# Batch 1's values loaded, copied and mixed earlier, and the third attention product ahead of the transposes

## The chip, the core and the metric

The kernel runs on one core of one Trainium2 chip. A core has a matrix engine (TensorE, PE in the profile; its weight loads are shown as PEld), a vector engine (VectorE, DVE), an activation engine (ScalarE, ACT), a general engine (GpSimd, POOL) and a queue engine (SyncE, SP). Each has its own instruction queue, and they wait for each other by semaphores. Transfers between device memory and on-chip memory are issued from SP's and POOL's queues and run on 16 DMA engines. The metric is the device time of one execution in microseconds, as the median over several runs. The time before is 253.93 us, the median of 9 runs (253.62 to 256.23).

## The reference: what is computed

Inputs are `q`, `k`, `v` of shape (4 batches, 8 heads, 768 positions, 64), a sorting matrix of 8x8 per batch and head, and three weights of an FFN (512 to 1536, gate and value, and 1536 to 512).

1. The 8x8 matrices are made nearly doubly stochastic by five rounds of: exponential, division by row sums, division by column sums. Call the result P.
2. The 768 positions are 8 blocks of 96. Keys and values are mixed over blocks: block i of the sorted keys is the sum over j of P[i,j] times block j, likewise for the values.
3. Each block of queries attends to the sorted keys and values of its own block: softmax(scale * q k^T) v, 96x96 scores per block and head.
4. The heads are laid side by side to x, 3072 tokens by 512, and the result is `(silu(x w_gate) * (x w_val)) w_out`, in float32.

## The kernel before, in words

Matrices are held in bfloat16; weights, keys, values and most queries are loaded and cast in one go by DMAs that POOL issues (`load_k`, `load_q`, `load_v`, `load_gv`, the latter two slices of 256 columns of gate and value weights). The order of those DMA issues is POOL's program order. POOL also does copies: `copy_v` rearranges a quarter of a batch's values in `v_tiles` to `vch`, with the head dimension outermost. Batches 0 and 1 share one such tile: batch 0 in the lower 64 partitions (`lowr`), batch 1 in the upper (`highr`). Batches 2 and 3 load into the same memory later, so their loads wait until batch 0's and batch 1's copies are done.

The mixing by P is done on PE: `kq_chunk` (matmuls at L235, tile `tkq`) multiplies 8 or 16 position columns of keys and queries at once by `rmix`, which also transposes them, and `v_chunk` (L247, tile `tv`) does the same for the values out of `vch`, by `vmix`. A value chunk covers a range of the head dimension and all 96 positions, so it needs all four quarters of the copy. Each chunk lands in a PSUM bank and is drained to on-chip memory by DVE ("v") or ACT ("s"), as its call names. PSUM tags are "a" and "b" (pairs of banks), "x" (one bank) and "gen" (a ring of three).

A unit of attention is two heads and four blocks: `qk` (scores L278, exponentials on ACT L291 or L289), `av` (L305, then a reciprocal and a product on DVE, L309 and L311, into `st`), and `x_to` (transposes, L322), drained into `xt`. A batch has 8 units; four units make one half batch of 384 tokens.

The FFN runs in 8 passes, one per half batch (`ffn(n)`). A pass has 12 chunks m of 128 hidden columns: `gate(n, m)` (L356, four matmuls of 384 columns), a tanh on ACT (L364) and a product on DVE (L366); `value(n, m)` (L374) and a product on DVE (L379); and, for the pass before it, three output projections `outp(n-1, t3, part)` (L391) of 128 tokens in three parts of four matmuls.

The order of PE and POOL is written out by hand. Until the first pass a straight list of calls is used: fillers on a zero tile (`fill`, L417), batch 0's value chunks, its key and query chunks, the four units of its first half with fillers between, and the first FFN matmuls taken apart by `early(n, kcs)` (L507: n = 0 and 1 are gate 0 and value 0, n = 2 is gate 1). From then on `merge(main, side)` walks through a pass's calls, adds up their costs (0.65 per gate or value, 0.87 per output part), and inserts a side call as soon as the sum reaches the number written beside it. `kqs`, `vs` and `units` make these side lists for a later half batch. DVE and ACT are also in written order until the first pass; after that a scheduler places them.

In the second pass (`ffn(1)`) the side work is batch 1's: three pairs of key and query chunks, four value chunks, then its first four units.

The rows behind `copy_v` for batch 1 on POOL are, before the change: `load_k_pair()` (keys of batches 2 and 3, into the buffer of batch 0's keys), the four copies, `load_v(2)`, `load_v(3)`, and two query casts into device memory (`q_cast`).

Of the kernel before, what the change touches and what calls it, by code (L numbers as in the profile page):

```python
# [17 lines left out]
def kernel(  # L18
# [15 lines left out]
    C = S // NB  # L34
# [5 lines left out]
    DF = moe_w_gate.shape[1]  # L40
    NKC = DM // 128
# [47 lines left out]
    def load_k(b, lo, hi):  # L89
        nc.gpsimd.dma_start(out=kq_tile(b)[0:R, lo:hi, :], in_=k_nat[b, :, lo:hi, :])  # L90

    def load_k_pair():
        kq_tiles["p"] = natp.tile([128, C, D], BF16, name="kp", tag="nat")
        for u in range(2):
            nc.gpsimd.dma_start(out=kq_tiles["p"][u * R:(u + 1) * R], in_=k_nat[2 + u])
# [4 lines left out]
    def load_v(b, lo, hi):  # L100
        if b // 2 not in v_tiles:
            v_tiles[b // 2] = vnp.tile([128, C, D], BF16, name=f"v{b // 2}", tag="vn")
        u = b % 2
        nc.gpsimd.dma_start(out=v_tiles[b // 2][u * R:(u + 1) * R, lo:hi], in_=v_nat[b, :, lo:hi, :])

    def load_w(sb, dram, lo, hi):
        nc.gpsimd.dma_start(out=sb[:, :, lo:hi], in_=dram[:, :, lo:hi])  # L107

    def load_gv(lo, hi):
        load_w(wg_sb, wg_dram, lo, hi)  # L110
        load_w(wv_sb, wv_dram, lo, hi)

    def copy_v(eng, pair, rows, s, n=4):
        cs = slice(s * (C // n), (s + 1) * (C // n))
        dst = vch3[rows, :, cs]
        src = v_tiles[pair][rows, cs, :]
        if eng is nc.scalar:
            eng.copy(dst, src.transpose([0, 2, 1]))
        else:
            eng.tensor_copy(dst, src.transpose([0, 2, 1]))  # L120
# [16 lines left out]
    copy_v(nc.gpsimd, 0, lowr, 3)  # L137
    landed = const.tile([R, 1], BF16)
    nc.gpsimd.tensor_copy(landed, kq_tiles[0][0:R, C - 1, D - 1:D])
    for m in range(0, DF, 256):  # L140
        load_gv(m, m + 256)
    load_k(1, 0, C)
    load_v(1, 0, C)
    load_q(1, 0, C)
    nc.gpsimd.dma_start(out=wo_sb, in_=wo_dram)

# [30 lines left out]
    def pair_tile(name, tag):  # L177
        return psum.tile([128, 1024], FP32, name=name, tag=tag)
# [24 lines left out]
    for lo in (0, NB // 2):  # L203
        part = slice(lo, lo + NB // 2)
# [89 lines left out]
    def qk(b, u, tag="b"):  # L294
        exps(b, u, *scores(b, u, tag))

    def av(b, u, tag="a"):
        half, g = divmod(u, H2)
        vt = vts[b // 2][:, b % 2].rearrange("p (h i) e -> p h i e", h=H)
        av_ps = pair_tile("av_ps", tag).rearrange("p (two n) -> p two n", two=2)  # L300
        o = av_ps[:, :, 0:4 * (D + 1)].rearrange("p two (i e) -> p two i e", e=D + 1)
        for two in range(2):
            e = es[(b, u)][two]
            for i4 in range(4):
                nc.tensor.matmul(o[:, two, i4, :], lhsT=e[:, i4 * C:i4 * C + 128],  # L305
                                 rhs=vt[:, 2 * g + two, half * 4 + i4, :],
                                 start=True, stop=True)
        r_sb = ssp.tile([C, 2, 4, 1], FP32, name="r_sb", tag="r")
        nc.vector.reciprocal(r_sb, o[0:C, :, :, D:D + 1])  # L309
        st = ssp.tile([C, 4, 2, D], BF16, name="st", tag="st")  # L310
        nc.vector.tensor_tensor(st.rearrange("p i two d -> p two i d"), o[0:C, :, :, 0:D],  # L311
                                r_sb.to_broadcast([C, 2, 4, D]), op=ALU.mult)
        sts[(b, u)] = st

    def xt_tile(tag, n):
        bank = psum.tile([128, 1024], BF16, name="x_ps", tag=tag, bufs=3 if tag == "gen" else 1)
        return bank[:, 0:n * 4 * C].rearrange("p (g a b) -> p g a b", g=n, b=C)
# [66 lines left out]
    def outp(n, t3, part):  # L384
        b, half = divmod(n, 2)
        h_w = h_tiles[n]
        if part == 0:
            o_tiles[n] = bank_tile("o_ps", "x" if 2 <= n < 2 * B - 1 or n == 2 * B - 1 and t3 == 1 else "gen")
        o_ps = o_tiles[n]
        for m in range(part * 4, part * 4 + 4):  # L390
            nc.tensor.matmul(o_ps, lhsT=h_w[:, m, ts(t3, 128)], rhs=wo_sb[:, m, :],  # L391
                             start=(m == 0), stop=(m == NFC - 1))
        if part < 2:
            return
        o_sb = opool.tile([128, DM], FP32, name="o_sb", tag="o_sb")
        nc.scalar.copy(o_sb, o_ps)  # L396
        base = b * S + half * TW + t3 * 128
        nc.sync.dma_start(out=out[ds(base, 128), :], in_=o_sb)
# [14 lines left out]
    idle_ps = bank_tile("idle_ps", "x")  # L413

    def fill(tile, n):
        for _ in range(n):
            nc.tensor.matmul(tile, lhsT=warm_sb[:, 0:128], rhs=warm_sb, start=True, stop=True)  # L417
# [37 lines left out]
    fill(idle_ps, 2)  # L455
    v_chunk(0, 0, 8, "v", "gen")
    v_chunk(0, 8, 16, "s", "a")
    fill(idle_ps, 2)
    v_chunk(0, 24, 16, "v", "b")
    fill(idle_ps, 2)  # L460
    v_chunk(0, 40, 8, "s", "gen")
    v_chunk(0, 48, 8, "v", "gen")
    v_chunk(0, 56, 8, "s", "gen")
# [17 lines left out]
    idle_ps = bank_tile("idle_ps")  # L481
# [3 lines left out]
    av(0, 1, "b")  # L485
    fill(idle_ps, 1)
    xts[(0, 0)] = xtp.tile([128, H2, TW], BF16, name="xt0_0", tag="xt")
    x01 = xt_tile("x", 2)
    x_to(x01[:, 0], 0, 0)
    fill(idle_ps, 1)  # L490
    qk(0, 3, "gen")
    av(0, 2, "a")
    x_to(x01[:, 1], 0, 1)
    drain("s", xts[(0, 0)][:, 0:2, :], x01.rearrange("p g a b -> p g (a b)"))
    fill(idle_ps, 2)
    av(0, 3, "b")
    x2 = xt_tile("gen", 1)
    x_to(x2[:, 0], 0, 2)
# [3 lines left out]
    def early(n, kcs):  # L502
        sb, m, name = ((wg_sb, 0, "g_ps"), (wv_sb, 0, "v_ps"), (wg_sb, 1, "g_ps"))[n]
        if n not in first:
            first[n] = psum.tile([128, TW], FP32, name=name, tag="gen", bufs=3)
        for kc in kcs:
            nc.tensor.matmul(first[n], lhsT=sb[:, kc, ts(m, 128)], rhs=xts[(0, 0)][:, kc, :],  # L507
                             start=(kc == 0), stop=(kc == NKC - 1))

    early(0, (0,))  # L510
    early(1, (0,))
    x3 = xt_tile("x", 1)
    x_to(x3[:, 0], 0, 3)
    drain("v", xts[(0, 0)][:, 3:4, :], x3.rearrange("p g a b -> p g (a b)"))
    early(0, (1, 2))
    early(1, (1, 2))
    early(0, (3,))
    early(1, (3,))
    early(2, range(NKC))
    gate_out(0, 0, first[0])  # L520
    value_out(0, 0, first[1])
    gate_out(0, 1, first[2])
# [5 lines left out]
    def units(b, us, ats):  # L528
        us = list(us)
        todo = []  # L530
        for n, at in enumerate(ats):
            u, u2 = us[2 * n:2 * n + 2]
            held = []
            todo.append((at, lambda u=u, u2=u2, held=held: (qk(b, u, "b"), held.append(scores(b, u2, "a")))))
            todo.append((at + 1.3, lambda u2=u2, held=held: exps(b, u2, *held[0])))
            for w, tag, t in ((u, "b", 1.9), (u2, "a", 3.6)):
                if b < 2:
                    todo.append((at + t, lambda w=w, tag=tag: av(b, w, tag)))
                    todo.append((at + t + 3.1, lambda w=w: drain("v", *xtr(b, w))))
                else:  # L540
                    todo.append((at + t, lambda w=w, tag=tag: (av(b, w, tag), x_dma(b, w))))
        return todo

    def kqs(b, ats):
        return [(at, lambda n=n: (kq_chunk(b, n * 32, 16, "v", "b"), kq_chunk(b, n * 32 + 16, 16, "s", "a")))
                for n, at in enumerate(ats)]

    def vs(f, size, ats):
        return [(at, lambda m=m: f(1, m * size, size, "sv"[m % 2], "ba"[m % 2])) for m, at in enumerate(ats)]

    def merge(main, side):
        done, k = 0.0, 0
        side = sorted(side, key=lambda t: t[0])
        for c, f in main:
            f()
            done += c
            while k < len(side) and side[k][0] <= done:
                side[k][1]()
                k += 1
        while k < len(side):  # L560
            side[k][1]()
            k += 1

    def ffn(n):
        todo = []
        for m in range(NFC):
            if n > 0 or m > 1:
                todo.append((0.65, lambda m=m: gate(n, m)))
            if n > 0 or m > 0:
                todo.append((0.65, lambda m=m: value(n, m)))  # L570
            if n > 0 and m % 4 == 3:
                for part in range(3):
                    todo.append((0.87, lambda m=m, part=part: outp(n - 1, m // 4, part)))
        return todo

    load_k_pair()
    for s in range(4):
        copy_v(nc.gpsimd, 0, highr, s)
    load_v(2, 0, C)
    load_v(3, 0, C)  # L580
    q_cast(2)
    q_cast(3)
    both = slice(0, 128)
    merge(ffn(0), units(0, range(4, 8), (0.0, 5.6)))
    merge(ffn(1), kqs(1, (0.3, 2.6, 4.9)) + vs(v_chunk, 16, (6.2, 7.3, 8.4, 9.5)) + units(1, range(4), (11.0, 15.6)))
    for s in range(4):
        copy_v(nc.gpsimd, 1, both, s)
    nc.vector.memset(kqt_tile("p")[:, 2 * GI * C:], 0.0)
# [42 lines left out]
```

The softmax here doesn't subtract the row's maximum and nothing guards it: scores larger than these inputs give would overflow.

## Time and profile before

The profiled execution took 254.17 us; the span from its first to its last instruction is 252.1 us, at a granted TensorE clock of 0.999 of full speed.

| engine | busy us | share of the span |
|---|---|---|
| PE | 238.3 | 95% |
| PEld | 143.2 | 57% |
| DVE | 159.4 | 63% |
| ACT | 110.6 | 44% |
| POOL | 51.9 | 21% |

The stages on PE, in us from the span's start: batch 0's value chunks 12.8 to 16.0, its key and query chunks 16.0 to 20.7, the first four units and the early FFN matmuls 21.6 to 30.3, the first pass from there to 47.5, the second pass 47.5 to 80.8, and six further passes and the last projections to 249.

Times of single instructions are "start, length"; matmuls are pipelined, so a group's length holds the latency of its last one, and the distance from one start to the next tells more (four matmuls of 384 columns go by in 0.65 us, four of 512 in 0.87, a key chunk of 64 matmuls in 1.13). An idle time in brackets is that of the engine just before the instruction, with what ended it; "issue" means that nothing shown by the profile did. For a DMA the trace gives the time of its issue and how long after that it landed. Some matmul records are missing, and a short idle time between fillers is mostly a missing filler.

### The profile page before, as it was taken

How to read it: one execution, taken by the hardware profiler on the slowest of the kernel's cores; microseconds unless marked ns; L12 is line 12 of the kernel's file. 1: busy time of each engine (PE TensorE's matmuls, PEld its weight loads, DVE VectorE, ACT ScalarE, POOL GpSimd, SP SyncE). 2: the span in 40 equal slices, each digit the busy share in tenths (PEclk: the TensorE clock that was granted, in tenths of full speed). 3: DMA queues.
4: the chain of work that ended last, by engine and by line, in shares of the span. 5: the costliest groups of instructions: out<-in, count | busy, mean ns of one | idle time of the engine just before them, and what ended most of it. 6: DMA issues, size and time to landing. Idle time of an engine off the chain costs nothing.

```text
span 252.1 us, 6035 instructions
## 1 busy us (share of the span) xinstructions
PE 238.3 (95%) x2548; PEld 143.2 (57%) x2574; DVE 159.4 (63%) x342; ACT 110.6 (44%) x187; POOL 51.9 (21%) x46
## 2 busy tenths in 40 slices
PE   5698799999999999999999999999999999999994
PEld 5275456566555565656656555555655565555543
DVE  6768588875756856758668457545854585456700
ACT  2965454346442443455543533443444343332311
POOL 7847430899069100000000000000000000000000
PEclk9999999999999999999999999999999999999999
DMA  6959999999999176110113122111211111100122
GB/s 104 210 96 159 197 219 219 189 221 218 223 158 144 42 175 123 44 42 3 42 26 80 42 51 52 46 44 33 61 56 42 34 57 57 44 11 30 44 83 85
DMA packets 37866, 23.98 MB, mean 95 GB/s; under 512 B 26064, under 2 KB 34000, under 8 KB 37328
## 3 DMA queue, kind: packets, MB, share of 16 engines
q0 software_dynamic: 21328, 14.16, 38.3%
q1 hardware_dynamic: 16512, 9.45, 13.0%
q8 instruction: 20, 0.33, 0.5%
q14 instruction: 6, 0.05, 0.1%
HBM read 28.32 MB, written 7.86 MB: 144 GB/s over the span
## 4 chain that ended last, share of the span: by engine, by line
PE 74%; DMA 15%; DVE 3%; POOL 3%; issue 2%; ACT 1%; DVEq 0%; POOLq 0%
PE o_ps L391 23%; PE v_ps L374 21%; PE g_ps L356 20%; DMA kq<-in_q_dram 7%; DMA kq<-in_k_dram 4%; DMA wg_sb<-in_moe_w_gate_dram 4%; PE tkq L235 3%; PE av_ps L305 2%; PE qk L278 2%; PE tv L257 1%; DVE gs_sb L366 1%; PE o_ps L407 1%; DVE vt L213 1%; POOL wg_sb L107 1%; POOL wv_sb L107 1%
## 5 line engine op out<-in xcount | busy, mean ns | idle before, releaser
L366 DVE SCALAR_TENSOR_TENSOR gs_sb<-th_sb,g_ps 128x384 bf16<-128x384 bf16 x96 | 52.8, 550 | 52.9 <-ACT th_sb L364 50.7
L374 PE MATMUL v_ps<-xt,wv_sb 128*128 128x384 bf16 x380 | 77.3, 326 | 0.3
L356 PE MATMUL g_ps<-xt,wg_sb 128*128 128x384 bf16 x376 | 76.5, 326 | 0.0
L364 ACT ACTIVATE th_sb<-g_ps 128x384 bf16<-128x384 f32 x96 | 47.1, 491 | 58.0 <-PE g_ps L356 54.9
L391 PE MATMUL o_ps<-wo_sb,h 128*128 128x512 bf16 x256 | 62.2, 379 | 1.1
L379 DVE SCALAR_TENSOR_TENSOR h<-v_ps,gs_sb 128x384 bf16<-128x384 f32 x96 | 53.3, 555 | 6.9 <-DVE gs_sb L366 0.5
L374 PEld LDWEIGHTS <-wv_sb 128*128 128x128 bf16 x380 | 35.4, 97 | 23.6 <-issue 1.5
L356 PEld LDWEIGHTS <-wg_sb 128*128 128x128 bf16 x376 | 34.6, 97 | 22.9 <-issue 0.2
L391 PEld LDWEIGHTS <-h 128*128 128x128 bf16 x276 | 26.0, 98 | 27.7
L396 ACT COPY o_sb<-o_ps 128x512 f32<-128x512 f32 x23 | 13.5, 585 | 51.4 <-PE o_ps L391 51.4
L120 POOL COPY vch<-v 64x1536 bf16<-64x1536 bf16 (+1 forms) x10 | 28.1, 2845 | 18.6 <-DMA v<-in_v_dram 10.4
L291 ACT ACTIVATE e_all<-qk 96x768 bf16<-96x768 f32 x30 | 22.5, 802 | 6.2 <-PE qk L278 6.2
L311 DVE TENSOR_TENSOR st<-av_ps,r_sb 96x512 bf16<-96x512 f32 x32 | 21.7, 679 | 0.2
L305 PEld LDWEIGHTS <-e_all 96*128 96x128 bf16 x256 | 12.2, 98 | 5.1 <-ACT e_all L291 0.9
L305 PE MATMUL av_ps<-vt,e_all 96*128 96x65 bf16 x256 | 13.5, 194 | 0.2 <-ACT e_all L291 0.2
L213 DVE CAST vt<-tv 96x1024 bf16<-96x1024 f32 (+1 forms) x9 | 9.8, 1101 | 4.3 <-PE tv L247 4.3
L215 ACT CAST vt<-tv 96x1024 bf16<-96x1024 f32 (+1 forms) x9 | 9.1, 1029 | 5.6 <-PE tv L247 2.9
L309 DVE RECIPROCAL r_sb<-av_ps 96x8 f32<-96x8 f32 x32 | 6.4, 199 | 7.1 <-PE av_ps L305 7.1
L235 PE MATMUL tkq<-rmix,kq 128*64 128x64 bf16 x384 | 7.6, 197 | 1.1 <-DMA kq<-in_q_dram 0.6
L215 ACT CAST kqt<-tkq 128x1024 bf16<-128x1024 f32 (+1 forms) x7 | 6.0, 894 | 5.7 <-PE tkq L235 5.7
L213 DVE CAST kqt<-tkq 128x1024 bf16<-128x1024 f32 (+1 forms) x7 | 7.5, 1070 | 1.2 <-PE tkq L235 1.1
L235 PEld LDWEIGHTS <-kq 128*64 128x64 bf16 x384 | 6.7, 113 | 2.4 <-issue 2.2
(79 smaller groups left out, 135.9 us busy)
## 6 DMA issues: line engine op xcount, KB each, us to landing
out_dram<-o_sb SPq DMA_DIRECT2D x23, 256.0 KB, 2.0
v<-in_v_dram POOLq DMA_DIRECT2D x3, 768.0 KB, 14.1
kq<-in_q_dram POOLq DMA_DIRECT2D x2, 768.0 KB, 13.4
wg_sb<-in_moe_w_gate_dram POOLq DMA_DIRECT2D x6, 256.0 KB, 9.6
wv_sb<-in_moe_w_val_dram POOLq DMA_DIRECT2D x6, 256.0 KB, 10.2
wo_sb<-in_moe_w_out_dram POOLq DMA_DIRECT2D x1, 1536.0 KB, 23.7
kp<-in_k_dram POOLq DMA_DIRECT2D x2, 768.0 KB, 27.0
q_scr<-in_q_dram POOLq DMA_DIRECT2D x2, 768.0 KB, 20.9
```

The costliest lines, as they stand in the source:

```text
L120: eng.tensor_copy(dst, src.transpose([0, 2, 1]))
L213: nc.vector.tensor_copy(dst, src)
L235: nc.tensor.matmul(tp[two * D:(two + 1) * D, lc, :], lhsT=kq_tiles[b][:, at + lc, :], rhs=rm[:, two, :], start=True, stop=True)
L291: nc.scalar.activation(e_all[:, n:n + 2, 0:4 * C], wide[0:C, :, 0:4 * C], AF.Exp, scale=scale)
L305: nc.tensor.matmul(o[:, two, i4, :], lhsT=e[:, i4 * C:i4 * C + 128], rhs=vt[:, 2 * g + two, half * 4 + i4, :], start=True, stop=True)
L311: nc.vector.tensor_tensor(st.rearrange("p i two d -> p two i d"), o[0:C, :, :, 0:D], r_sb.to_broadcast([C, 2, 4, D]), op=ALU.mult)
L356: nc.tensor.matmul(g_ps, lhsT=wg_sb[:, kc, ts(m, 128)], rhs=xt[:, kc, :], start=(kc == 0), stop=(kc == NKC - 1))
L364: nc.scalar.activation(th_sb, g_ps, AF.Tanh, scale=0.5)
L366: nc.vector.scalar_tensor_tensor(gs_sb, th_sb, 1.0, g_ps, op0=ALU.add, op1=ALU.mult)
L374: nc.tensor.matmul(v_ps, lhsT=wv_sb[:, kc, ts(m, 128)], rhs=xt[:, kc, :], start=(kc == 0), stop=(kc == NKC - 1))
L379: nc.vector.scalar_tensor_tensor(h_tiles[n][:, m, :], v_ps, 0.5, gs_tiles.pop(m), op0=ALU.mult, op1=ALU.mult)
L391: nc.tensor.matmul(o_ps, lhsT=h_w[:, m, ts(t3, 128)], rhs=wo_sb[:, m, :], start=(m == 0), stop=(m == NFC - 1))
```

## The change

On POOL, batch 1's value load moves from behind the third key load to ahead of the last two pairs of weight slices (the last four of twelve weight DMAs), and the four copies move ahead of `load_k_pair()`. On PE, six fillers go: four among batch 0's value chunks and two among the first units. The scores of unit 3 and the third `av` move ahead of the first transposes. The early FFN matmuls are taken in another order: two contraction chunks of gate 0 and value 0 ahead of the last transposes, one of gate 1 between the others. In the second pass the value chunks come first and the key and query chunks after them, the units start 0.3 and 0.2 later in the list's costs, and the output projections of the first half batch follow chunks 5, 8 and 11 instead of 3, 7 and 11.

```diff
     nc.gpsimd.tensor_copy(landed, kq_tiles[0][0:R, C - 1, D - 1:D])
-    for m in range(0, DF, 256):
+    for m in range(0, 1024, 256):
+        load_gv(m, m + 256)
+    load_v(1, 0, C)
+    for m in range(1024, DF, 256):
         load_gv(m, m + 256)
     load_k(1, 0, C)
-    load_v(1, 0, C)
     load_q(1, 0, C)
     nc.gpsimd.dma_start(out=wo_sb, in_=wo_dram)
...
     v_chunk(0, 0, 8, "v", "gen")
     v_chunk(0, 8, 16, "s", "a")
-    fill(idle_ps, 2)
     v_chunk(0, 24, 16, "v", "b")
-    fill(idle_ps, 2)
     v_chunk(0, 40, 8, "s", "gen")
...
     xts[(0, 0)] = xtp.tile([128, H2, TW], BF16, name="xt0_0", tag="xt")
+    qk(0, 3, "gen")
+    av(0, 2, "a")
     x01 = xt_tile("x", 2)
     x_to(x01[:, 0], 0, 0)
-    fill(idle_ps, 1)
-    qk(0, 3, "gen")
-    av(0, 2, "a")
     x_to(x01[:, 1], 0, 1)
     drain("s", xts[(0, 0)][:, 0:2, :], x01.rearrange("p g a b -> p g (a b)"))
-    fill(idle_ps, 2)
+    fill(idle_ps, 1)
     av(0, 3, "b")
...
-    early(0, (0,))
-    early(1, (0,))
+    early(0, (0, 1))
+    early(1, (0, 1))
     x3 = xt_tile("x", 1)
     x_to(x3[:, 0], 0, 3)
     drain("v", xts[(0, 0)][:, 3:4, :], x3.rearrange("p g a b -> p g (a b)"))
-    early(0, (1, 2))
-    early(1, (1, 2))
+    early(0, (2,))
+    early(1, (2,))
+    early(2, (0,))
     early(0, (3,))
     early(1, (3,))
-    early(2, range(NKC))
+    early(2, (1, 2, 3))
...
-            if n > 0 and m % 4 == 3:
+            ends = (5, 8, 11) if n == 1 else (3, 7, 11)
+            if n > 0 and m in ends:
                 for part in range(3):
-                    todo.append((0.87, lambda m=m, part=part: outp(n - 1, m // 4, part)))
+                    todo.append((0.87, lambda t3=ends.index(m), part=part: outp(n - 1, t3, part)))
...
-    load_k_pair()
     for s in range(4):
         copy_v(nc.gpsimd, 0, highr, s)
+    load_k_pair()
     load_v(2, 0, C)
...
-    merge(ffn(1), kqs(1, (0.3, 2.6, 4.9)) + vs(v_chunk, 16, (6.2, 7.3, 8.4, 9.5)) + units(1, range(4), (11.0, 15.6)))
+    merge(ffn(1), vs(v_chunk, 16, (2.2, 3.1, 4.0, 4.9)) + kqs(1, (5.8, 8.0, 10.2)) + units(1, range(4), (11.3, 15.8)))
```

## The prediction, made before the changed kernel was run

> **What bounds the kernel now.** I read the page's busy line first, then busy time by stage, then TensorE's (PE's) timeline where a stage holds less work than it lasts, then the waits and GpSimd's (POOL's) timeline.
>
> The page's first line, then the stages (us, busy time per engine, granted clock, DMA share, GB/s):
>
> ```profile
> PE 238.3 (95%) x2548; PEld 143.2 (57%) x2574; DVE 159.4 (63%) x342; ACT 110.6 (44%) x187; POOL 51.9 (21%) x46
> ...
> 12.60:16.00 3.40, 3.11 (x68) 2.26 (x68) 1.91 (x3) 1.77 (x4) 0.12 (x1) 1.00 0.65 123
> 16.00:21.60 5.60, 4.93 (x198) 3.94 (x199) 4.52 (x7) 3.88 (x6) 5.60 (x9) 1.00 0.81 97
> 21.60:30.30 8.70, 6.90 (x99) 4.20 (x101) 5.14 (x16) 4.90 (x9) 4.44 (x7) 1.00 1.40 189
> 30.30:47.40 17.10, 16.96 (x165) 10.57 (x164) 14.93 (x35) 8.07 (x15) 4.89 (x5) 1.00 1.17 209
> 47.40:80.80 33.40, 32.33 (x468) 20.27 (x470) 23.61 (x44) 14.78 (x24) 24.98 (x12) 1.00 1.48 200
> 80.80:252.00 171.20, 166.87 (x1416) 97.16 (x1431) 100.69 (x196) 69.15 (x121) 1.86 (x1) 1.00 0.19 53
> ```
>
> From 30.3 on PE is the bound: the end moves by as much as the first full pass starts earlier, less what is lost later. Only the stages before 80.8 are changed. In 12.6 to 30.3 much of PE's time is filler; this is where most can be won. The attention start:
>
> ```profile
> 25.07 0.43 PE L305 MATMUL av_ps<-vt,e_all 96*128 96x65 bf16 x8
> 25.34 0.24 PE L322 MATMUL x_ps<-ident,st 96*128 96x96 bf16 x2
> 26.52 0.26 PE L322 MATMUL x_ps<-ident,st 96*128 96x96 bf16 x2 [0.94 <-issue]
> 26.61 0.60 PE L417 MATMUL idle_ps<-warm_sb 128*128 128x512 bf16 x2
> 27.05 0.42 PE L305 MATMUL av_ps<-vt,e_all 96*128 96x65 bf16 x8
> ...
> q8 instruction: 1, 0.02, 5.4%
> ```
>
> PE stops in the middle of four transposes whose data is there, released by nothing (issue). The last line, the DMA view of 24.2 to 25.3 alone, shows a packet of PE's code starting then; the page has 20 such of 16 KB for PE's 5,161 instructions, so one per 256. I read the stop as PE out of code. Waits in 47 to 81, and the four second-half copies on POOL:
>
> ```profile
> PE tkq L235 <- DMA kq<-in_q_dram: 0.6, 1, 0.6
> PE qk L278 <- DVE vt L213: 0.3, 1, 0.3
> ...
> 45.11 11.24 POOL L120 COPY vch<-v 64x1536 bf16<-64x1536 bf16 x4 [9.63 <-DMA v<-in_v_dram]
> ```
>
> **Part 1, up to the first scores.** Four fillers between the value chunks go. Two such (14.68) take 0.54 to the next chunk's start at 15.22, the first pair 0.69 (an idle 0.16 in it): 1.23 together. The key chunks then wait for bank "a", whose ScalarE (ACT) drain runs 13.68 + 1.06 = 14.74; so they start at 14.8 instead of 16.02: **1.2**. All later drains follow PE at the same distance, so the 1.2 lasts to the third AV. Key loads are not in the way: the last lands at 15.83, and its chunk (19.78) comes at 18.5. Bounds: 0.7 (the first pair alone) to 1.6 (if an extra 0.25 idle at 17.2 and at 19.5 shrinks too).
>
> **Part 2, third AV ahead of x.** Before, the first matmul of plain FFN order (L374) starts at 30.30; the fourth AV starts 0.53 after the stop ends (26.52 to 27.05: half a transpose group, two fillers), and L374 3.25 after that. Counting 256 instructions on from the stop's place, the next block of code again ends inside this group, now two matmuls into the fourth AV, with transposes and third AV already behind it; so the 0.53 goes. From the fourth AV on: its last transposes start +1.44 (27.05 to 28.49), the key matmuls behind their drain +0.83 (28.49 to 29.32), then five matmuls at 0.163 = 0.82: 3.09 instead of 3.25, 0.16 won. If the code arrives 1.2 earlier too, because its request was made 1.2 earlier: 1.2 + 0.53 + 0.16 = **1.9** for parts 1 and 2. Bounds: code no earlier than now, since the queues carry the same weights then: 0.7. No stop at all: the AV waits for the exps, which start 0.37 after the scores (24.80 to 25.17) and take 0.86; scores now at 23.1 (third exps end 24.26 - 1.2), AV 24.4, L374 27.5: 2.8. I take 1.9, the value nearest the one stop the trace has.
>
> The Trainium skill ("Runtime: NRT & Kernel Launch", Instruction fetch mechanics) says code comes in 16 KiB blocks, PE's store holds 2048 instructions and a block's crossing is mostly hidden. The 0.94 row contradicts the last point; by the rule alone there would be no stop afterwards and the sum would be the 2.8 case, near 251.0.
>
> **Part 3, loads.** On POOL's queue the ninth issue (21.96) and each later one wait for the landing eight before; single issues landed at 21.7, 23.0, 24.5, 26.8, 28.0, 29.4, 30.6, 32.0 (weights), 33.3, 34.6, 36.1, 38.0, then third key 41.0, value 45.0, query 48.7, output weights 55.9. They land in issue order; so the moved value load takes its 3.0 to 4.0 at 32.0 and lands at 35 to 36; the last four weight slices land up to 4.0 later (37.3, 38.6, 40.1, 42.0), the key at 45, query and output weights unchanged. First needs before: gate 8 at 41.53, value 8 at 42.17, gate 10 at 44.56, value 10 at 45.35; less 1.9: 39.6, 40.3, 42.7, 43.4. Each covered, by 1.4 at the least; cost 0. Copies 36 to 47.3 (11.24). The pair load, two values and two query casts that queue behind the copies on POOL are issued from 47.3, while output weights are in flight to 55.9: the queue never empties, cost 0. VectorE (DVE) beside copies: L366 means 550 ns in 45.2 to 56.3, 545 in 31 to 45; L379 553 and 555; so no charge to the first pass, where DVE is busy 14.93 of 17.1.
>
> **Part 4, second pass** (starts 47.47 - 1.9 = 45.6). Work is unchanged, only its order. Gone: 0.72 before the key chunk (48.12 to 48.84; chunk now near 53.4, query 48.7), 0.38 before the scores (65.22 to 65.60, a DVE cast), 0.29 in two shorter ones beside the key chunks: 1.4. First value chunk at 48.2, copies done 47.3: covered by 0.9. Output weights (55.9) wanted at about 57.6: covered. New: value chunks no longer lie between output projections. Within three gate/value pairs (3.9 us of PE) DVE gets two casts of 1.22 more, and the fourth cast stands behind two of its own pairs. The second half of the first key chunk needs that bank. Now the fourth value chunk starts 63.14 and its cast ends 65.55, 2.41 on; in the new order the bank is wanted 0.47 + 0.65 + 0.57 = 1.69 on: 0.7 by that row, 1.1 with the second cast's backlog counted, 1.6 if both casts stand ahead in full. I take **1.1**, and 0.1 for code (rival A). Net 0.2 won (0.7 to -1.2). SyncE's queue (output stores, query transposes) keeps its order and is later needed with over 10 us in hand. Six fillers fewer are counted in parts 1 and 2.
>
> **Sum.** The profiled execution took 254.17 (span 252.1, 2.1 around it), 0.24 over the median. 254.17 - 1.9 - 0.2 = 252.1; on the median's footing 251.9.
>
> **Rivals.**
> A, slower: code starves PE in the second pass. In the new order 256 instructions pass between the first and second key chunk groups in 6 to 7 us. Blocks under full DMA come slowly: the one stop ended about 7.5 after PE entered the block before. Against: at 49 to 63 today PE runs the same mix without such a stop. At 7.5 the wait is 0 to 1; it decides from a cycle of about 9, two blocks 1.5 late each with the early stop ending no sooner: 254.5 to 255.5. Chance 0.12.
> B: the early stop vanishes: 252.1 - 0.9, on the median 251.0. For it, one stop in 20 blocks; against, the same code distance. 0.11.
> C: the code's arrival is fixed by the weights, not by the request: 0.7 instead of 1.9, part 4 anywhere in its range: 252.9 to 253.9. 0.19, about a third of it within 0.3% of before.
> D: the change does not do what it says: the value load does not land before the later weights. From 38 its copies are late (49.2 against 48.2); landing at 45.0 as now, PE waits 8: 260. Against, the landing order. 0.04.
>
> **Numbers.** Forecast 0.54, own range 251.3 to 252.8. Measurement tells 0.3% (0.8 us). Faster: 0.54 + 0.11 + 0.12 of C = 0.77; same 0.07 + 0.02 of A = 0.09; slower 0.10 + 0.04 = 0.14. Range 250.7 (B, with part 4 at its best) to 253.9 (end of C); A's and D's tails are left out.
>
> **What would show it.** Key chunks start near 14.8; the stop's end near 25.3, inside the fourth AV; first L374 matmul near 28.4; POOL's copies begin near 36; no PE wait for the query; a PE wait of about 1 for the DVE value cast in the first key chunk; first output matmul after 55.9 with no wait; from the third pass on the old distances. I am wrong if L374 still starts after 29.6, if a second stop on issue appears near 56 to 64, or if the value load lands after 38.

## The result, and the profile after

The changed kernel takes 252.11 us, the median of 12 runs (251.23 to 253.43); the kernel before, run beside it, 254.28 (39 runs, 253.29 to 257.05). The ratio is 0.9902, with a 95% interval of 0.9874 to 0.9931. It is the quotient of the means, 252.25 and 254.74, not of the medians: nine of the 39 executions before took 256.2 to 257.1, which the median does not show. The profiled execution took 251.46, with a span of 249.5, against 254.17 and 252.1. The forecast was 251.9 (250.7 to 253.9).

The page's first line after, and then the same stages as before (us, busy time per engine, granted clock, DMA share, GB/s):

```profile
PE 238.0 (95%) x2542; PEld 143.2 (57%) x2568; DVE 159.4 (64%) x342; ACT 110.6 (44%) x187; POOL 52.0 (21%) x46
```

```profile
12.60:16.00 3.40, 3.29 (x129) 3.17 (x129) 2.61 (x4) 2.51 (x4) 0.00 (x0) 1.00 0.66 125
16.00:20.30 4.30, 3.72 (x134) 2.82 (x134) 3.57 (x4) 2.89 (x4) 3.91 (x7) 1.00 0.66 81
20.30:28.60 8.30, 7.82 (x117) 4.85 (x117) 6.08 (x18) 5.50 (x11) 5.73 (x8) 1.00 1.34 175
28.60:45.60 17.00, 16.86 (x158) 10.50 (x152) 14.85 (x36) 7.77 (x15) 12.21 (x7) 1.00 1.23 214
45.60:78.00 32.40, 31.32 (x459) 19.55 (x462) 22.94 (x43) 14.73 (x23) 15.23 (x10) 1.00 1.39 204
78.00:249.40 171.40, 167.16 (x1418) 97.30 (x1432) 100.70 (x196) 69.06 (x121) 4.83 (x2) 1.00 0.24 56
```

PE's busy time is the same; the attention start (third row) now has 7.82 of 8.30 us busy, where it had 6.90 of 8.70. So idle time was won, as was meant, and it was won early. The milestones of the two profiled executions say where (us from the span's start, each the start of a matmul on PE):

| milestone | before | after | earlier by |
|---|---|---|---|
| first key chunk of batch 0 | 16.02 | 14.73 | 1.29 |
| first scores | 21.61 | 20.50 | 1.11 |
| first FFN matmul in plain order (L374, now L376) | 30.30 | 27.49 | 2.81 |
| second pass | 47.47 | 44.67 | 2.80 |
| third pass | 80.78 | 78.28 | 2.50 |
| span | 252.1 | 249.5 | 2.6 |

The first pass lasts 17.17 and 17.18 us. From the third pass to the end it is 171.3 and 171.2. All that was gained lies before the first plain pass, and 0.3 of it was lost again in the second pass.

The attention start after the change, on PE's timeline (start, length, matmuls), and the DMA view of 21.2 to 22.3, where the packet of PE's code now starts:

```profile
23.45 0.43 PE L307 MATMUL av_ps<-vt,e_all 96*128 96x65 bf16 x8
23.72 0.65 PE L324 MATMUL x_ps<-ident,st 96*128 96x96 bf16 x8
24.43 0.42 PE L307 MATMUL av_ps<-vt,e_all 96*128 96x65 bf16 x8
...
27.49 0.81 PE L376 MATMUL v_ps<-xt,wv_sb 128*128 128x384 bf16 x4
```

```profile
q8 instruction: 1, 0.02, 5.1%
```

All eight transposes go in one piece and the fourth AV follows: the stop of 0.94 us has no successor. The code packet starts at 21.37, where it started at 24.24 before: 2.87 earlier.

The second pass: POOL's copies, and PE's timeline where it waits.

```profile
35.51 11.22 POOL L120 COPY vch<-v 64x1536 bf16<-64x1536 bf16 x4 [2.63 <-DMA v<-in_v_dram]
```

```profile
47.31 0.63 PE L249 MATMUL tv<-vmix,vch 128*128 128x64 bf16 x16
52.69 0.69 PE L237 MATMUL tkq<-rmix,kq 128*64 128x64 bf16 x32
53.74 0.70 PE L237 MATMUL tkq<-rmix,kq 128*64 128x64 bf16 x32 [0.36 <-DVE vt L215]
```

```profile
57.51 1.20 PE L237 MATMUL tkq<-rmix,kq 128*64 128x64 bf16 x64
58.87 1.67 PE L393 MATMUL o_ps<-wo_sb,h 128*128 128x512 bf16 x7 [0.16 <-issue]
60.47 1.20 PE L237 MATMUL tkq<-rmix,kq 128*64 128x64 bf16 x64
...
62.27 1.10 PE L376 MATMUL v_ps<-xt,wv_sb 128*128 128x384 bf16 x4
```

The value load landed early, the copies ran from 35.51 to 46.73, and the first value chunk (47.31) and the first key chunk (52.69) wait for nothing. The second half of the key chunk waits for the fourth value cast. Measured against the distance from one start to the next where nothing waits, that wait is 0.48. The same reckoning gives 0.21 at 56.54, for the output weights, and 0.30 around 62.27, with no releaser; there 990 weight loads lie ahead, which will turn out to be the end of a block of code. The idle 0.16 shown at 58.87 is no wait. Eight matmuls stand there in the program and seven are recorded, the weight load of the first started on time at 58.64, and the distance between the two key chunks around them (57.51 to 60.47) is 2.96 to 2.97 in all seven profiles with this order.

### The profile page after: what moved, and what is told of

Same layout as the page of the kernel before. It is cut to its first block, busy times and chain, and to the rows that moved or that the text cites. A ratio compares the mean times of both kernels' runs of the same rounds, so it can differ in the third digit from the quotient of the medians.

```text
span 249.5 us, 6025 instructions
## 1 busy us (share of the span) xinstructions
PE 238.0 (95%) x2542; PEld 143.2 (57%) x2568; DVE 159.4 (64%) x342; ACT 110.6 (44%) x187; POOL 52.0 (21%) x46
## 4 chain that ended last, share of the span: by engine, by line
PE 85%; DVE 6%; ACT 3%; issue 3%; DMA 2%; DVEq 0%; ACTq 0%; POOLq 0%
PE v_ps L376 24%; PE g_ps L358 23%; PE o_ps L393 22%; PE tkq L237 4%; PE av_ps L307 3%; PE qk L280 2%; DMA v<-in_v_dram 2%; DVE h L381 2%; DVE gs_sb L368 1%; PE tv L259 1%; PE tv L249 1%; PE o_ps L409 1%; DVE st L313 1%; PE x_ps L324 1%; ACT e_all L293 1%
## 5 line engine op out<-in xcount | busy, mean ns | idle before, releaser
L368 DVE SCALAR_TENSOR_TENSOR gs_sb<-th_sb,g_ps 128x384 bf16<-128x384 bf16 x96 | 52.8, 550 | 53.4 <-ACT th_sb L366 51.1
L376 PE MATMUL v_ps<-xt,wv_sb 128*128 128x384 bf16 x380 | 77.5, 326 | 0.4
L381 DVE SCALAR_TENSOR_TENSOR h<-v_ps,gs_sb 128x384 bf16<-128x384 f32 x96 | 53.3, 556 | 6.8 <-DVE gs_sb L368 0.5
L376 PEld LDWEIGHTS <-wv_sb 128*128 128x128 bf16 x380 | 35.6, 97 | 24.0 <-issue 1.6
L358 PEld LDWEIGHTS <-wg_sb 128*128 128x128 bf16 x376 | 34.5, 97 | 22.6 <-issue 0.2
L398 ACT COPY o_sb<-o_ps 128x512 f32<-128x512 f32 x23 | 13.4, 585 | 48.9 <-PE o_ps L393 48.9
L120 POOL COPY vch<-v 64x1536 bf16<-64x1536 bf16 (+1 forms) x10 | 28.1, 2853 | 20.5 <-PE g_ps L358 17.2
## 6 DMA issues: line engine op xcount, KB each, us to landing
wo_sb<-in_moe_w_out_dram POOLq DMA_DIRECT2D x1, 1536.0 KB, 24.7
kp<-in_k_dram POOLq DMA_DIRECT2D x2, 768.0 KB, 14.8
```

What stands on the lines that cost most here:

```text
L358: nc.tensor.matmul(g_ps, lhsT=wg_sb[:, kc, ts(m, 128)], rhs=xt[:, kc, :], start=(kc == 0), stop=(kc == NKC - 1))
L368: nc.vector.scalar_tensor_tensor(gs_sb, th_sb, 1.0, g_ps, op0=ALU.add, op1=ALU.mult)
L376: nc.tensor.matmul(v_ps, lhsT=wv_sb[:, kc, ts(m, 128)], rhs=xt[:, kc, :], start=(kc == 0), stop=(kc == NKC - 1))
L381: nc.vector.scalar_tensor_tensor(h_tiles[n][:, m, :], v_ps, 0.5, gs_tiles.pop(m), op0=ALU.mult, op1=ALU.mult)
```

## The experiments

Two theories stood at the outset. The first: the early gain is larger than forecast because PE's code was requested earlier and came earlier still, so that the stop vanished; it hangs on the four fillers between the value chunks. The second: it was the new order of the third AV, the transposes and the early FFN matmuls that took the stop away, wherever the code was. A further question was what each half of the change, the early part and the values, is worth alone.

### One half alone

The early part alone, on the kernel before:

```diff
     v_chunk(0, 8, 16, "s", "a")
-    fill(idle_ps, 2)
     v_chunk(0, 24, 16, "v", "b")
-    fill(idle_ps, 2)
...
+    qk(0, 3, "gen")
+    av(0, 2, "a")
     x01 = xt_tile("x", 2)
     x_to(x01[:, 0], 0, 0)
-    fill(idle_ps, 1)
-    qk(0, 3, "gen")
-    av(0, 2, "a")
...
```

The sixth filler and the order of the early FFN matmuls are as in the change too; loads, copies and the second pass are as before.

> The kernel before with the change's early part alone: six fillers out, third AV ahead of the transposes, early FFN matmuls in the new order; loads, copies and the second pass as before. Theory 1 (the halves need each other): the first plain value matmul (L374) starts near 27.5 as in the changed kernel, the second pass near 44.7, but its first key chunk then waits for the query that lands at 48.7, some 3.4 us; the end stays where it was, 0 to 0.5 us faster. Theory 2 (the gains add): the early 2.8 us reach the end, about 2.5 us faster.

Measured: L374 at 27.55, so the whole early gain of 2.75 is there. But the time is 255.64 (ratio 1.0016, 0.9979 to 1.0054): nothing is left of it. The timeline of the second pass's start and the busy time of two windows:

```profile
49.02 1.20 PE L235 MATMUL tkq<-rmix,kq 128*64 128x64 bf16 x64 [3.48 <-DMA kq<-in_q_dram]
```

```profile
48.00:50.00 2.00, 0.98 (x63) 1.01 (x64) 0.25 (x1) 0.00 (x0) 2.00 (x1) 1.00 1.27 208
50.00:54.00 4.00, 4.00 (x32) 1.75 (x27) 2.11 (x5) 1.50 (x2) 4.00 (x3) 0.57 1.27 215
```

PE comes to the key chunk 2.75 earlier and the query lands when it did (48.9, before 48.7), so PE sits idle for 3.48 where it did for 0.56; from one start to the next the wait is 3.65 against 0.72. After that idle time the granted clock falls to half, from 50.4, for 3.4 us (0.57 in the second window). So the second pass is longer by more than the wait: 37.92 us against 33.31, 4.61 longer, of which the wait explains 2.93. That leaves 1.68.

The values alone (load order, copies, second pass), with the early part as before:

```diff
-    for m in range(0, DF, 256):
+    for m in range(0, 1024, 256):
+        load_gv(m, m + 256)
+    load_v(1, 0, C)
+    for m in range(1024, DF, 256):
         load_gv(m, m + 256)
     load_k(1, 0, C)
-    load_v(1, 0, C)
...
```

The copies ahead of `load_k_pair()` and the lists of the second pass are as in the change too.

> The changed kernel with the early part as before: only the value load and copies moved, and the second pass in the new order. Theory 1: the second pass starts at 47.5 as before; no query wait (0.72 gone) and no wait for the output weights, but a wait of 0.5 for the fourth value cast; second pass 33.0 to 33.5 against 33.3 before; the end moves by no more than 0.4 us either way. Theory 2 (the new order pays by itself): waits of 1.4 go and nothing takes their place, 1 to 1.4 us faster.

Measured: 253.76, ratio 0.9946 (0.9909 to 0.9984). The profiled execution, the longest of its ten, shows no gain in the span (252.2) and a second pass of 34.05; the ratio says some 1.4 us, with an interval of 0.4 to 2.3. That leaves both expectations open, and the profile shows one reason for the spread, a stop at an end of a block of code (PE timeline):

```profile
25.33 0.25 PE L324 MATMUL x_ps<-ident,st 96*128 96x96 bf16 x2
25.96 0.26 PE L324 MATMUL x_ps<-ident,st 96*128 96x96 bf16 x2 [0.39 <-issue]
...
29.74 0.81 PE L376 MATMUL v_ps<-xt,wv_sb 128*128 128x384 bf16 x4
...
64.47 0.19 PE L237 MATMUL tkq<-rmix,kq 128*64 128x64 bf16 x1 [0.78 <-issue]
```

The two ratios multiply to 0.996; together the halves give 0.990. So about 0.6% comes from the halves being together; by the three intervals it could be anything from nothing to 1.2%, so that the halves need each other rests on the wait of 3.48 more than on this sum. The early part brings PE to the second pass before the query is there, and the values give PE something to do until it is.

### The fillers and PE's code

Only the four fillers out of the kernel before, with its order of AV and transposes kept:

```diff
     v_chunk(0, 8, 16, "s", "a")
-    fill(idle_ps, 2)
     v_chunk(0, 24, 16, "v", "b")
-    fill(idle_ps, 2)
     v_chunk(0, 40, 8, "s", "gen")
```

> The kernel before without the four fillers among the value chunks, nothing else. Theory 1 (code is asked for earlier and then stands behind fewer weight transfers): the code packet that started at 24.2 starts at 21 to 22; no stop in the transposes; key chunks 1.2 earlier, L374 near 28.1, 2.1 or 2.2 earlier; the end unchanged, since the query wait grows to about 2.9. Theory 2 (the packet starts when the weight traffic lets it, whatever the request): packet near 24.2, stop until about 26.5, L374 at 30.0 to 30.3.

And the same four put back into the changed kernel, at the same places:

```diff
     v_chunk(0, 8, 16, "s", "a")
+    fill(idle_ps, 2)
     v_chunk(0, 24, 16, "v", "b")
+    fill(idle_ps, 2)
     v_chunk(0, 40, 8, "s", "gen")
```

> The changed kernel with the four fillers among the value chunks put back. Theory 1: the request for code is as late as before, so the packet starts near 24 and PE stops at the fourth AV until about 26.5; L374 near 29.5, 2.0 later than in the changed kernel, and the end 1.5 to 2 us later than it. Theory 2 (the stop has nothing to do with when code is asked for; the new order of AV and transposes removes it): L374 1.2 later, near 28.7, the end 0.8 to 1.2 us later.

Measured, without the fillers: the key chunks start at 14.80, the code packet at 21.90, there is no stop at the transposes (a short one of 0.23 stands one block of code earlier, at 18.44), and L374 starts at 28.39, 1.9 earlier than before. The time (255.5, one execution) is no gain, for the same reason as above: the query is waited for, and the clock falls, here after 2.41 us only.

```profile
48.79 1.92 PE L235 MATMUL tkq<-rmix,kq 128*64 128x64 bf16 x64 [2.41 <-DMA kq<-in_q_dram]
```

With the fillers back in the changed kernel the stop is back too, though the third AV stands ahead of the transposes (PE timeline):

```profile
24.62 0.61 PE L324 MATMUL x_ps<-ident,st 96*128 96x96 bf16 x7
25.97 0.22 PE L324 MATMUL x_ps<-ident,st 96*128 96x96 bf16 x1 [0.75 <-issue]
...
29.31 0.81 PE L376 MATMUL v_ps<-xt,wv_sb 128*128 128x384 bf16 x4
```

The code packet starts at 23.62, and L376 at 29.31, 1.8 later than in the changed kernel, while the fillers themselves are worth some 1.2. The time is 252.96, one execution. The first theory holds: four fillers carry the stop with them in both orders. The new order of AV, transposes and early FFN matmuls does not remove it. L376 is 0.99 earlier than before (30.30 to 29.31), but 0.55 of that is code that came earlier (PE goes on at 25.97 instead of 26.52). Beside the kernel with the values alone, which has the old order and goes on at 25.96, the order is worth 0.43 (29.74 to 29.31).

Where the stop falls could now be counted. In the kernel before, in the values alone and in the one with the fillers back, 478 weight loads lie ahead of it, wherever in the order that is: after two transposes of a group of four, or after seven of eight. That is the end of a block of code. About the 350th, 128 matmuls of two instructions ahead, is where PE enters that block. Times of four places:

| kernel | PE enters the block | its successor's packet starts | PE reaches the 478th | PE goes on | stop |
|---|---|---|---|---|---|
| before | 19.03 | 24.24 | 25.4 | 26.52 | 0.94 |
| values alone | 18.95 | 23.59 | 25.4 | 25.96 | 0.39 |
| four fillers back | 18.96 | 23.62 | 25.0 | 25.97 | 0.75 |
| four fillers out | 17.99 | 21.90 | 24.7 | 24.7 | none |
| changed | 17.92 | 21.37 | 24.4 | 24.4 | none |

PE goes on 2.3 to 2.4 us after the packet's start. The packet starts 3.5 to 5.2 us after PE enters the block (without the fillers counted from 18.44, where PE goes on after the short stop), and that delay is the larger part and differs from kernel to kernel. With 2.35 after the packet, the code is there at 24.25 without the fillers and at 23.7 in the changed kernel, 0.4 and 0.7 ahead of PE.

The pair of runs is one profile each, but all profiles agree with it. The three with the four fillers at their places (before, values alone, fillers back) have the packet at 23.59 to 24.24 and stop at the 478th. The nine without the four fillers, of which the rest follow below, have it at 20.76 to 23.11, and none stops there for more than 0.2. The gain isn't safe, though: five of the nine stop one block earlier instead, after the 351st weight load among batch 0's key chunks, for 0.23 to 0.67, and the later work keeps that delay.

Two shifts of the blocks against the work were to test the count:

```diff
-    for _ in range(114):
+    for _ in range(134):
```

> The kernel before with 134 instead of 114 of the tiny filler matmuls at its start, where TensorE waits for the first values anyway; nothing else. Each is two instructions, so a place counted in instructions from the start moves 20 matmuls back in the written order. Theory 1 (the stop is the end of a block of code that has not come): the stop leaves the second transposes and is found 20 matmuls earlier in the order, at the filler behind the first four transposes, reached at about 24.6 and held until about 26; the scores and exps of unit 3 then start late and L374 is at 30.5 to 31. Theory 2 (the stop belongs to the transposes or to a data wait the profile does not name): it stays between the second and the third of the second four transposes, L374 near 30.3.

```diff
-    for _ in range(114):
+    for _ in range(204):
...
-    fill(idle_ps, 6)
+    fill(idle_ps, 1)
```

> The kernel before with 204 instead of 114 tiny fillers and one instead of six fillers behind them: 85 matmuls more, so that the block's end falls into the first pass, reached at about 31 when its code has long come. Theory 1: no stop in 24 to 29 at all, L374 near 29.4, 0.9 earlier; the end unmoved, since the query still lands at 48.7 and TensorE waits 1.6 for it in place of 0.7. Theory 2: the stop stays at the transposes, L374 near 30.3.

The first is inconclusive: in that run the granted clock stood at half from 12.3 to 22.6, all later work came some 3 us late, and PE reached the block's end at 28.5, about when its code came (packet at 26.15, and 2.35 on is 28.5). There was no stop, but this run can't tell the shift from the delay. The time is 256.63, one execution. The busy time of that stretch (the column after POOL's is the clock):

```profile
16.00:22.00 6.00, 5.53 (x128) 4.48 (x128) 3.14 (x3) 2.36 (x4) 6.00 (x10) 0.50 0.92 114
```

The second gave the opposite of what I had written down. I had put the block's end in the first pass; but the added matmuls move the same 478th matmul of the program into the key chunks, where PE came to it at 20.5, earlier than ever, and waited longest (PE timeline):

```profile
19.94 0.72 PE L235 MATMUL tkq<-rmix,kq 128*64 128x64 bf16 x33 [0.25 <-issue]
23.36 0.41 PE L235 MATMUL tkq<-rmix,kq 128*64 128x64 bf16 x15 [2.70 <-issue]
```

A stop of 2.70 stands after 33 matmuls of a chunk whose data was there, 479 weight loads on from the start, 2.4 after a code packet that starts at 20.96. The miss is the better evidence: the stop goes with the count of instructions and not with the work. After it the clock falls to half again (24.1 to 27.5), and L374 starts at 32.91. The time is 256.44, one execution.

### The clock after the wait for the query

To show that the fall of the clock is the price beyond the wait, fifteen fillers were put ahead of the first key chunk of batch 1 in the kernel with the early part alone:

```diff
+    def warm(b, n):
+        if b == 1 and n == 0:
+            fill(pair_tile("warm", "b")[:, 0:512], 15)
...
-        return [(at, lambda n=n: (kq_chunk(b, n * 32, 16, "v", "b"), kq_chunk(b, n * 32 + 16, 16, "s", "a")))
+        return [(at, lambda n=n: (warm(b, n), kq_chunk(b, n * 32, 16, "v", "b"), kq_chunk(b, n * 32 + 16, 16, "s", "a")))
```

> The early part alone once more, now with 15 full fillers in the second pass just ahead of the first key chunk, where TensorE sat idle for 3.5 us and its granted clock then fell to 0.5 for 3.4 us. Theory 1 (the idle time, not the work, halves the clock): the clock stays at 1.0, the key chunk still starts near 49.0, and the second pass ends some 1.6 earlier than without the fillers; the time is 0.3 to 0.6% below the kernel before. Theory 2 (the clock falls for another reason, such as the load then): the clock falls again near 50 and the time is that of the early part alone, 0 to 0.4% over before.

```profile
46.00:50.00 4.00, 3.49 (x16) 1.47 (x16) 1.23 (x3) 0.49 (x1) 4.00 (x2) 1.00 1.17 178
50.00:54.00 4.00, 3.99 (x126) 3.00 (x128) 2.53 (x5) 1.50 (x2) 4.00 (x2) 1.00 1.26 211
```

The clock stays at full speed, and from that key chunk to the third pass it is 31.94 us (50.01 to 81.95), as in the kernel before, instead of 33.62: 1.68 less, which is what the wait had left unexplained. The executions of the early part alone say the same without a profile: eight of the ten had a mean clock of 0.986 to 0.993 and took 255.0 to 256.4, the other two had 1.000 and took 253.8 and 254.0. The time is still no better (254.49, ratio 1.001, 0.9982 to 1.0038), against an expected 0.3 to 0.6% below. In this profile the query landed at 49.9 instead of 48.9 and ate 1.0 of it; that this holds for all its executions is not shown, and why the fillers don't pay in the time is open.

### The second pass of the changed kernel

The changed kernel once more, without an edit, beside the following three on one chip:

> The changed kernel again, for the three that follow: 0.988 to 0.993 of the kernel before; second pass about 33.6, with the wait of about 0.5 for the fourth value cast and waits of 0.2 to 0.4 for code and for the output weights.

Measured 252.58, ratio 0.9898 (0.9853 to 0.9943). Its profiled execution is the longest of its six (253.14), and shows what can spread them: the early part is the same to 0.01 us (L376 at 27.50), the second pass lasts 35.23 instead of 33.61. PE's waits from 44.7 to 79.9 (us, count, longest):

```profile
PE v_ps L376 <- issue: 0.9, 1, 0.9
PE o_ps L393 <- DMA wo_sb<-in_moe_w_out_dram: 0.9, 1, 0.9
PE tkq L237 <- DVE vt L215: 0.4, 1, 0.4
PE o_ps L393 <- issue: 0.2, 1, 0.2
```

A stop for code of 0.89 at 64.35 and a wait of 0.85 for the output weights at 57.41, both of which were 0.2 to 0.3 in the other profile. The last row is the missing record again.

The fourth value cast moved from DVE to ACT takes away the one wait that both profiles share:

```diff
-        return [(at, lambda m=m: f(1, m * size, size, "sv"[m % 2], "ba"[m % 2])) for m, at in enumerate(ats)]
+        return [(at, lambda m=m: f(1, m * size, size, ("svss" if f is v_chunk else "svsv")[m % 4], "ba"[m % 2])) for m, at in enumerate(ats)]
```

> The changed kernel with the fourth value chunk of batch 1 drained by ScalarE instead of VectorE. Theory 1 (the second half of the first key chunk waits for VectorE's backlog of two casts): that wait, 0.48 from start to start, shrinks below 0.1, and the second pass takes 33.1 to 33.3 instead of 33.6; time 0.1 to 0.2% below the changed kernel. Theory 2 (ScalarE's queue takes its place, since the next tanh stands behind the cast): the pass stays at 33.5 to 33.8.

> The fourth value cast on ScalarE again, now beside the changed kernel on one chip. If the cast's wait is what the second pass lost: second pass 32.7 to 33.0, 0.2 to 0.4% below the changed kernel. If the better time of the first such run was the chip's or the code packets' luck: equal to it within 0.1%.

```profile
53.11 1.26 PE L237 MATMUL tkq<-rmix,kq 128*64 128x64 bf16 x64
```

The key chunk goes in one piece, and the second pass lasts 32.80 in the first profile and 33.04 in the second. The times are 251.07 (ratio 0.9878, 0.9838 to 0.9918) and, beside the changed kernel on one chip, 251.93 against 252.58 (0.9887, 0.9836 to 0.9938, against 0.9898). The wait is gone from the profile; in the time it can't be told from the changed kernel.

On top of that, the key chunks and units were spread further, with the output projections after chunks 6, 9 and 11:

```diff
-            ends = (5, 8, 11) if n == 1 else (3, 7, 11)
+            ends = (6, 9, 11) if n == 1 else (3, 7, 11)
...
-    merge(ffn(1), vs(v_chunk, 16, (2.2, 3.1, 4.0, 4.9)) + kqs(1, (5.8, 8.0, 10.2)) + units(1, range(4), (11.3, 15.8)))
+    merge(ffn(1), vs(v_chunk, 16, (2.2, 3.1, 4.0, 4.9)) + kqs(1, (5.8, 8.4, 11.4)) + units(1, range(4), (12.4, 16.2)))
```

> The fourth cast on ScalarE, and the second pass's key chunks at 5.8, 8.4, 11.4, units at 12.4 and 16.2, output projections behind chunks 6, 9 and 11. If code packets limit where three key chunks lie close (stops of 0.2 to 0.4 between 58 and 63): these go, second pass 32.3 to 32.6, 0.1 to 0.2% below the run with the cast alone. If not: 32.8 and the same time, or up to 0.4 worse, since the last transposes now stand just ahead of the third pass.

```profile
47.97 0.64 PE L249 MATMUL tv<-vmix,vch 128*128 128x64 bf16 x16 [0.48 <-POOL vch L120]
...
70.32 0.34 PE L280 MATMUL qk<-kqt 64*128 64x96 bf16 x8 [0.94 <-DVE st L313]
```

The stop for code near 63 and the wait for the output weights are gone, but the units, now closer together, wait 0.94 for DVE, and this time the copies were late by 0.48. The pass lasts 34.05; 252.28, ratio 0.9896 (0.9854 to 0.9938): no gain.

Last, the kernel with the cast on ACT and the three single fillers among batch 0's key chunks out as well:

```diff
     kq_chunk(0, 16, 16, "s", "b")
-    fill(idle_ps, 1)
     kq_chunk(0, 32, 8, "s", "gen")
...
     kq_chunk(0, 48, 8, "v", "gen")
-    fill(idle_ps, 1)
     kq_chunk(0, 56, 16, "v", "b")
-    fill(idle_ps, 1)
     kq_chunk(0, 72, 16, "s", "a")
```

> The fourth cast on ScalarE, and the three single fillers among batch 0's key chunks out. If these are on the path as the four among the value chunks were: scores 0.3 to 0.9 earlier, then the first value chunk of batch 1 meets the end of its copies (46.7) and gives part of it back; 0 to 0.2% below the run with the cast alone. If the drains of the key chunks set the pace: scores at the same time, no gain.

```profile
20.39 0.69 PE L280 MATMUL qk<-kqt 64*128 64x96 bf16 x24 [0.49 <-DVE kqt L215]
...
56.91 1.04 PE L393 MATMUL o_ps<-wo_sb,h 128*128 128x512 bf16 x3 [1.01 <-DMA wo_sb<-in_moe_w_out_dram]
```

The first scores come only 0.1 earlier, since PE now waits 0.49 for a drain that the fillers covered, and the output weights are waited for by 1.01. The time is 251.57, ratio 0.987 (0.983 to 0.991), the lowest on that chip, but its interval overlaps that of the changed kernel.

## Why the prediction was right, and where it was not

The time, 251.9 forecast and 252.11 measured, is right, and so is the reason: idle time of PE before the first pass. But two terms were off, by 0.9 and 0.5 in opposite directions, so that the two figures lie within 0.2 of each other is in part luck.

**Part 1** was right: key chunks at 14.73 against 14.8.

**Part 2** is the term that was mis-sized: 1.9 for parts 1 and 2, measured 2.81. The step is "If the code arrives 1.2 earlier too, because its request was made 1.2 earlier". The direction held, the size did not: the request came 1.1 earlier (19.03 to 17.92) and the packet 2.9, because the delay between the two fell from 5.2 to 3.5. So the stop did not end at 25.3, it did not happen, and 2.8, the upper bound of that part (rival B), is what was measured, to the place (fourth AV at 24.43, L376 at 27.49). That size isn't certain in every execution: of five profiles with the same code up to L376, three have it at 27.5, the other two, with stops one block earlier, at 27.92 and 28.44, which is 2.4 and 1.9 won. The new order's own share, 0.53 and 0.16 in the forecast, came to 0.43 where both orders have the stop. The reading of the stop as PE out of code is shown by the count of 478 and by the shift of 85. Why the delay differs is not: that a code packet queues among the weight transfers fits, and was not tried. "One stop in 20 blocks" was a weak reason against rival B: the margin was never looked at.

The Trainium skill ("Runtime: NRT & Kernel Launch", Instruction fetch mechanics) holds that crossing a block is mostly hidden. By that rule the stop is an exception; here it appeared at the same count in four of fourteen profiles, from 0.39 to 2.70 us, and one block earlier in five others, from 0.23 to 0.67; its absence in the changed kernel had a margin of 0.7.

**Part 3** was right in each row: copies from 35.51 to 46.73 (forecast 36 to 47.3), no wait of the first pass, which kept its 17.2 us, and DVE undisturbed by the copies (L368 took 546 ns in the mean beside them, L381 550). One of its covers was too thin: the output weights, "wanted at about 57.6: covered". With the early part 0.9 faster than forecast they were wanted at 56.3 and landed at 56.5, and in two other profiles PE waited 0.85 and 1.01.

**Part 4** was forecast at 0.2 won and measured at 0.30 lost. What was to go went (no wait for the query, none for the copies). The new wait for the fourth cast was taken at 1.1 and measured at 0.48, below the lower bound of 0.7: PE had the bank 2.26 after the fourth chunk's start, sooner than the 2.41 of the row that the bound was taken from, and the second cast's backlog added nothing to it. In exchange, things booked at 0.1 or nothing came to more: 0.30 for the end of a block of code, 0.21 for the output weights, and some 0.7 in three short waits (50.8, 66.2, 69.7) that the forecast did not name. By these rows it is 1.4 gone and 1.7 new: 0.3 lost, as the pass shows.

**Rival A** has the right mechanism at too high a price: a stop on issue did appear near 62.7, and at 64.35 in the second profile, which by the letter of the last sentence on what would be wrong counts against the forecast. It cost 0.3 and 1.0, less than the early gain. **C** is excluded by the four-filler pair and by the nine and three profiles counted above: the arrival of the code follows the request. **D** did not occur.

What the forecast did not see is that the halves depend on each other. It booked 0.72 for the query's wait as gone; the early half without the values would have turned that into 3.65 and a clock at half, and gained nothing.

## What to carry to other kernels

A gain made early is only kept if the next thing that PE waits for from memory is not then met sooner: look at the first load that PE already waits for, and move work that needs nothing from it ahead of it. A stop of PE with no releaser can be tested by counting instructions from the start; if the count stays the same while the work under it changes, the cure is to reach it later or to ask for the code earlier, and a few fillers taken out ahead of the request can be worth more than their own time. Look at the block's end before it as well, where the stop may turn up instead. When a wait of half a microsecond is removed in a stage that is full, look for the two next ones behind it before counting it as won.

## What the runs showed of the hardware that was not expected

The granted clock fell to half after idle times of 2.41, 2.70 and 3.48 us, and each time stayed there for 3.41 us. The fall does not follow the wait at once: it came 12, 5 and 13 whole times 3.41 us after the clock's first rise in these runs, 0 to 1.4 us after PE went on, and in the 3.41 us ahead of it PE had been idle for 2.4, 2.7 and 2.0. The Trainium skill ("TensorE: Matmul & The Clock Gate", HAM oscillation) warns of idle gaps above about 3.4 us; here 2.41 was enough, and 0.94 was not. The kernel before may lose the same way now and then: of its 43 executions beside the experiments ten had a mean clock of 0.993, which is what one such fall makes of 252 us, and took 255.8 to 257.0, the other 33 took 253.3 to 255.7; none of the ten was profiled. In the run with twenty more matmuls at the start the clock was at half for 10.2 us (12.3 to 22.6), three times as long, while the longest idle time shortly ahead of it was 1.85, ended 2.3 us earlier; the cause is open.

For the same order of issues, loads land up to 2 us apart from run to run: in the eight profiles with the changed order of loads the query landed between 47.9 and 49.4 and the output weights between 55.2 and 57.4. In a stage where PE meets several of them with little in hand, that moves the end: PE's wait for the output weights was 0.21, 0.85 and 1.01 in three of them. Code does the same: with the same code up to L376, both profiles of the changed kernel start it at 27.49 and 27.50, the one with the units spread at 27.51, and those with the cast on ACT alone at 27.92 and 28.44, after stops of 0.31 and 0.67 at the end of the block before (the 351st weight load).
